# Linear attention with a highway layer on one core: softmax work of batches 2 and 3 moved, x added on GpSimd, output tiles as fp16 transposes

## Chip, core and metric

The kernel runs on one core of a Trainium2 chip. The metric is the device time of one execution in microseconds (us). A core has five engines with instruction queues of their own, each worked off in order: TensorE (PE, matrix products; its weight loads are PEld), VectorE (DVE), ScalarE (ACT), GpSimd (POOL) and SyncE (SP, which here only issues transfers). They wait for one another through semaphores. SBUF is the working memory of 128 partitions, PSUM the memory that PE writes to.

## What is computed

q, k and v have 8 batches, 8 heads, 576 rows and 64 columns. The result of the attention is, row by row, the input x of a highway layer with two 512 x 512 weight matrices.

```
q_s = exp(q) / sum over the 64 columns         # softmax of each row of a head
k_s = exp(k) / sum over the 576 rows
kv  = einsum('bhsd,bhse->bhde', k_s, v)        # one 64 x 64 matrix per head
x   = einsum('bhsd,bhde->bhse', q_s, kv)       # as 4608 rows of 512
H   = max(x @ w_h, 0)
T   = sigmoid(x @ w_t + b_t)
out = T * H + (1 - T) * x
```

Inputs and output are float32. Inside, the kernel works in fp16 with sums in fp32.

## The kernel before

**Layout.** A partition holds 9 consecutive rows (n = 0 to 8) of half of the heads, so a batch's q, k or v is one tile of 128 partitions x 2304 elements (1152 KB). A "half" a is half of the heads (1152 elements). x is kept transposed: xT[g] holds two batches (a group g) with the 512 model columns in four blocks of 128 (index k_ or ob) and rows n = 0 to 7. The ninth rows of all batches are collected in x9 and handled as a ninth "batch" at the end.

**Attention part of a batch b.** exp_half (L150) is the exponential on ACT, for q into eq and for k into ek. q_sums (L195) sums eq's rows on DVE, q_recip (L203) takes the reciprocals, and eq is scaled by them on GpSimd (q_scale_p, L214; the first 1024 elements, then 1280) or on DVE (q_scale_v, L206, which first widens the reciprocals, L210, and then multiplies, L212). cast_v (L160) brings half of v to fp16 on GpSimd. q_trans (L218) transposes scaled eq on PE in three pieces into PSUM (pq), copied to qsT on DVE (L233). kv_half (L167) is 36 small products of ek and v into psk; kv_norm (L183) divides by the key sums on DVE (rz, kvn). x_pair (L235) and x_left (L259) are the products px and px_l that give x; of an x_pair's copies into xT three of four are on ACT (L255), one on DVE (L257).

**Highway part of batch c and output block ob.** gate (L283) is four products with w_t into pt and a tanh on ACT in place. carry (L291) is four products with w_h into ph, then dd = max(ph, 0) - x on DVE (L297). blend (L302) is g = (tanh + 1) * dd on DVE (L305); since sigmoid(z) = (1 + tanh(z/2))/2, the output is x + g/2. out_tile (L321) brings one n of a group back to rows on PE: turn_block (L313) multiplies x by an identity and adds g times half an identity, both into fp32 PSUM (nat), eight products in all; ACT copies 512 elements (L336, in the last group every second tile on DVE, L334), and every fourth tile is followed by a transfer of 1 MB (L339). most9 and last9 (L347, L361) do the same for the ninth rows.

**Order.** The order of every queue is written out by hand. A list (L427 on) gives the start: batches 0 and 1 of attention, the weights, the four gates and carries of batch 0, and the loads of batches 2 and 3. After it, time runs in half steps p = 8 to 72, and `at(p, ...)` puts work on a half step. In each batch of 8 half steps a gate is at the even and a carry at the odd ones; blend(c, ob) is two half steps after its gate. The attention of batch b is placed relative to p = 8(b-1), where the gates of batch b-1 begin (L397 to L423). What is put on one half step is issued in the order in which it was put there, and each engine runs its share in that order.

**Buffers.** PSUM has four tiles for pt and ph (`ps_ht`), three for pq, psk, px and px_l (`ps_q`, in rotation) and one for nat (`ps_nat`). eq and ek have two buffers, q, k and v three each as loaded.

Of the kernel before, what the change touches and what calls it, by code (L numbers as in the profile page):

```python
# [18 lines left out]
def kernel(  # L19
# [86 lines left out]
    def cast_weight(n, k_, eng):  # L106
        o, i = w16[n][:, k_], w32[n][:, k_]
        if eng is nc.scalar:
            eng.copy(o, i)
        else:  # L110
            eng.tensor_copy(o, i)
# [47 lines left out]

    def cast_v(b, a, eng=None):  # L160
# [34 lines left out]
    def q_sums(b, a):  # L195
        if a == 0:
            qsum[b] = small.tile([P, N9, 4], FP32, tag="r32", name=f"r32_{b}")
        h = slice(2 * a, 2 * a + 2)
        nc.vector.reduce_sum(qsum[b][:, :, h], eq[b][:, :, h, :], axis=AX.X)  # L199

# [90 lines left out]
    def carry(c, ob):  # L291
        xv = views(c)[0]
        ps = ps_ht.tile([P, 8, 64], FP32, tag="ht", name=f"ph_{c}_{ob}")
        for k_ in range(4):
# [3 lines left out]
            dd, ps, 0.0, xv(ob), op0=ALU.max, op1=ALU.subtract  # L298
# [10 lines left out]

    o32 = {}  # L310
    rows = out.rearrange("(g p n) m -> g p n m", g=B // 2, n=N9)

    def turn_block(t, k_, xs, us):  # L313
        dst = t[:, k_, :]
        mm(dst, xs, ident, True, False)
        mm(dst, us, half_i, False, True)
# [4 lines left out]
    def out_tile(g, n, spare=False):  # L321
        if n % 4 == 0:
            o32[g, n // 4] = og.tile([P, 4, 512], FP32, tag="o32", name=f"o32_{g}_{n}")
        ps, tag = (ps_q, "qx") if spare and n % 4 < 3 else (ps_nat, "nat")
        t = ps.tile([P, 4, P], FP32, tag=tag, name=f"nat_{g}_{n}")
        for k_ in range(4):
            turn_block(
                t, k_,
                xT[g][:, k_, n].rearrange("p b d -> p (b d)"),
                gT[g][:, k_, n].rearrange("p b d -> p (b d)"),  # L330
            )
        o = o32[g, n // 4][:, n % 4, :]
        if spare and n % 2:
            nc.vector.tensor_copy(o, flat(t))  # L334
        else:
            nc.scalar.copy(o, flat(t))  # L336
        if n % 4 == 3:
            i = n // 4
            nc.sync.dma_start(rows[g][:, 4 * i : 4 * i + 4, :], o32[g, i])  # L339
# [43 lines left out]
    for c in range(1, B + 1):  # L383
        for ob in range(4):
            at(8 * c + 2 * ob + 2, E(blend, c, ob))

    for g in range(B // 2):
        p = 16 * (g + 1)
        if g < B // 2 - 1:
            for i in range(8):  # L390
                at(p + 2 + 2 * i, E(out_tile, g, i))
        else:
            for i in range(8):
                at(p + 1 + i // 2, E(out_tile, g, i, True))
    at(8 * B + 8, E(most9), E(last9))

    for b in range(2, B):  # L397
        p = 8 * (b - 1)
        s = p + {2: 0, 3: -4}.get(b, -5)
        at(s, E(exp_half, b, "q", 0))  # L400
        at(s + 1, E(exp_half, b, "q", 1), E(q_sums, b, 0))
# [88 lines left out]
```

## Time and profile before

| | us |
|---|---|
| median of 13 runs (148.53 to 151.34) | 149.09 |
| profiled execution, its own time | 149.08 |
| its span, first to last instruction | 146.9 |
| PE busy (share of the span) | 123.2 (84%) |
| DVE busy | 108.1 (74%) |
| ACT busy | 87.3 (59%) |
| POOL busy | 43.2 (29%) |
| mean granted TensorE clock | 0.966 |

The span leaves out 2.18 us that lie around the instructions. Busy times of engines overlap, so they don't add up to the span; a row such as "L216 POOL TENSOR_TENSOR eq<-eq,r" is a group of instructions by line, engine, operation and tiles, with total busy time and the mean of one. What an engine waited for is named by the instruction that released it. Matmuls are pipelined, so the mean duration of one (219 ns for 128 columns) is longer than the spacing of two that follow one another (0.056 us in the timeline).

### The profile page before, as it was taken

The page shows a single profiled execution, that of the slowest core. Times are in us where ns is not written, and L with a number is a line of the kernel's source. Part 1 is how long each engine was busy: PE and PEld are TensorE (multiplying, and loading weights), DVE is VectorE, ACT ScalarE, POOL GpSimd, SP SyncE. Part 2 cuts the span into 40 slices and gives each one's busy share as a digit, 9 for nine tenths or more (in the row PEclk, how much of TensorE's full clock was granted, in tenths as well). Part 3 has the DMA queues.
Part 4 walks back from the last instruction along what each step waited for, and adds up shares of the span by engine and source line. Part 5 has one row for each costly group of instructions (what it writes and reads, how often), then busy time and mean ns, then how long its engine had stood idle before and what let it go on. Part 6 is the DMA issues. An engine that isn't in the chain of part 4 may idle for free.

```text
span 146.9 us, 3530 instructions
## 1 busy us (share of the span) xinstructions
PE 123.2 (84%) x1477; PEld 67.9 (46%) x1477; DVE 108.1 (74%) x201; ACT 87.3 (59%) x126; POOL 43.2 (29%) x37
## 2 busy tenths in 40 slices
PE   4979999688528979979999599959977999999920
PEld 1335345234124436636645364634645455577620
DVE  1493589975997988996899389929983767577750
ACT  3650658336980269798499539936980764465420
POOL 2006011600084069059207900970295000000000
PEclk9999999999965999999999999999999999999995
DMA  4999999999999999403999999630051006047745
GB/s 156 354 383 408 410 391 410 412 413 405 412 408 411 407 411 411 173 0 140 271 407 414 324 405 407 280 154 0 4 225 62 4 0 285 0 174 319 297 176 181
DMA packets 16022, 40.06 MB, mean 273 GB/s; under 512 B 644, under 2 KB 1672, under 8 KB 14984
## 3 DMA queue, kind: packets, MB, share of 16 engines
q1 hardware_dynamic: 16008, 39.85, 70.6%
q8 instruction: 11, 0.18, 0.5%
q14 instruction: 3, 0.02, 0.0%
HBM read 30.41 MB, written 9.44 MB: 271 GB/s over the span
## 4 chain that ended last, share of the span: by engine, by line
PE 45%; DVE 29%; ACT 6%; POOL 6%; issue 4%; DMA 3%; POOLq 3%; SPq 0%; DVEq 0%; ACTq 0%
PE ph L59 14%; PE pt L59 12%; DVE r L199 10%; PE nat L59 6%; DVE dd L297 4%; PE psk L59 4%; POOL eq L216 3%; DVE eq L212 3%; DMA q<-in_q_dram 3%; DVE g L305 3%; POOLq L485 3%; PE pq L64 3%; PE px L59 3%; PE warm L59 3%; DVE qsT L233 2%
## 5 line engine op out<-in xcount | busy, mean ns | idle before, releaser
L288 ACT ACTIVATE pt<-pt,bt 128x512 f32<-128x512 f32 x36 | 24.0, 669 | 36.1 <-PE pt L59 35.7
L216 POOL TENSOR_TENSOR eq<-eq,r 128x1024 f16<-128x1024 f16 (+1 forms) x11 | 22.9, 2097 | 47.2 <-DVE r L204 34.6
L297 DVE SCALAR_TENSOR_TENSOR dd<-ph,xT 128x512 f16<-128x512 f32 x32 | 21.9, 684 | 16.9 <-PE ph L59 16.9
L59 PE MATMUL ph<-xT,w16h 128*128 128x512 f16 x128 | 33.7, 388 | 0.0
L59 PE MATMUL pt<-xT,w16t 128*128 128x512 f16 x128 | 32.9, 381 | 0.0
L305 DVE SCALAR_TENSOR_TENSOR g<-pt,dd 128x512 f16<-128x512 f32 x36 | 24.5, 681 | 1.9
L199 DVE TENSOR_REDUCE r<-eq 128x18 f32<-128x1152 f16 x16 | 21.6, 1348 | 4.4 <-ACT eq L154 4.1
L161 POOL CAST v<-v 128x1152 f16<-128x1152 f32 x16 | 18.6, 1185 | 13.8 <-DMA v<-in_v_dram 13.8
L154 ACT ACTIVATE ek<-k 128x1152 f16<-128x1152 f32 x16 | 18.6, 1184 | 2.5 <-DMA k<-in_k_dram 2.5
L154 ACT ACTIVATE eq<-q 128x1152 f16<-128x1152 f32 x16 | 18.4, 1171 | 2.6 <-DMA q<-in_q_dram 2.6
L59 PEld LDWEIGHTS <-w16t 128*128 128x128 f16 x144 | 12.8, 98 | 14.2 <-issue 1.1
L59 PE MATMUL nat<-half_i,g 128*128 128x128 f16 x140 | 18.7, 219 | 0.0
L59 PEld LDWEIGHTS <-w16h 128*128 128x128 f16 x144 | 12.4, 99 | 12.1 <-issue 1.7
L336 ACT COPY o<-nat 128x512 f32<-128x512 f32 x28 | 16.9, 602 | 1.7 <-issue 1.1
L64 PE MATMUL pq<-ident,eq 128*128 128x128 f16 x144 | 12.8, 231 | 6.0 <-POOL eq L216 4.1
L255 ACT CAST xT<-px 128x512 f16<-128x512 f32 x24 | 13.4, 596 | 7.2 <-PE px L59 7.1
L59 PE MATMUL nat<-ident,xT 128*128 128x128 f16 x128 | 17.3, 219 | 0.0
L59 PE MATMUL warm<-wide,ident 128*128 128x512 f16 x52 | 15.2, 441 | 1.9 <-DVE wide L140 1.9
L59 PEld LDWEIGHTS <-g 128*128 128x128 f16 x144 | 14.1, 98 | 3.8 <-DVE g L305 0.4
L64 PEld LDWEIGHTS <-eq 128*128 128x128 f16 x144 | 9.9, 103 | 9.8 <-POOL eq L216 4.6
L59 PEld LDWEIGHTS <-xT 128*128 128x128 f16 x128 | 12.5, 98 | 3.3
L59 PE MATMUL psk<-v,ek 64*64 64x65 f16 x576 | 8.1, 197 | 6.8 <-POOL v L161 5.5
(42 smaller groups left out, 91.7 us busy)
## 6 DMA issues: line engine op xcount, KB each, us to landing
out_dram<-o SPq DMA_DIRECT2D x8, 1024.0 KB, 4.3
q<-in_q_dram SPq DMA_DIRECT2D x7, 1152.0 KB, 13.4
k<-in_k_dram SPq DMA_DIRECT2D x7, 1152.0 KB, 14.3
v<-in_v_dram SPq DMA_DIRECT2D x6, 1152.0 KB, 14.7
v<-in_v_dram SPq DMA_DIRECT2D x4, 576.0 KB, 10.8
q<-in_q_dram SPq DMA_DIRECT2D x2, 576.0 KB, 4.1
k<-in_k_dram SPq DMA_DIRECT2D x2, 576.0 KB, 7.4
w32t<-in_moe_w_t_dram SPq DMA_DIRECT2D x1, 1024.0 KB, 13.7
```

Of the source, the lines that this page charges most:

```text
L59: mm = lambda o, l, r, st, sp: nc.tensor.matmul(o, l, r, start=st, stop=sp, skip_group_check=True)
L64: nc.tensor.matmul(o, i, ident, is_transpose=True, start=True, stop=True, skip_group_check=True,)
L154: nc.scalar.activation(dst[b][:, :, 2 * a : 2 * a + 2, :], in32[which][b][:, 2 * a : 2 * a + 2].rearrange("p c n d -> p n c d"), AF.Exp,)
L161: (eng or nc.gpsimd).tensor_copy(v16s[b % 2][:, :, 2 * a : 2 * a + 2, 0:64], in32["v"][b][:, 2 * a : 2 * a + 2].rearrange("p c n d -> p n ...
L199: nc.vector.reduce_sum(qsum[b][:, :, h], eq[b][:, :, h, :], axis=AX.X)
L212: nc.vector.tensor_mul(e, e, r2.unsqueeze(2).broadcast_to([P, w, 32, 2]))
L216: nc.gpsimd.tensor_mul(e, e, r.broadcast_to(list(e.shape)))
L255: nc.scalar.copy(dst, t[c])
L288: nc.scalar.activation(ps, ps, AF.Tanh, bias=bt2[:, ob : ob + 1], scale=0.5)
L297: nc.vector.scalar_tensor_tensor(dd, ps, 0.0, xv(ob), op0=ALU.max, op1=ALU.subtract)
L305: nc.vector.scalar_tensor_tensor(gv(ob), th, 1.0, dd, op0=ALU.add, op1=ALU.mult)
L336: nc.scalar.copy(o, flat(t))
```

## The change

1. **Weights.** w_h becomes (w_h - I)/2: four subtractions of the 128 x 128 identity blocks on DVE, and the casts on GpSimd and ACT multiply by 0.5.
2. **Carry.** dd = max(-x/2, ph), which with the new weights is half of the old dd. g is then the whole difference between output and x.
3. **add_x.** g += x on GpSimd, one instruction of 512 elements for each block of batches 0 to 7, one half step after its blend.
4. **Output.** out_pair replaces out_tile: two n at a time, eight fp16 transposes of g into one fp16 PSUM tile, one copy of 1024 elements, on ACT or, in the last group, every second one on DVE. The ninth rows keep two products each, with the whole identity.
5. **Softmax.** From batch 3 on, exp_all does a whole tile at once and q_sums_all sums by two fp16 additions and a reduction of the last 16 columns. All scales of batches 2 and up are on GpSimd.
6. **Order.** Batch 2's exponentials of q start ahead of the half steps, its v is cast half on GpSimd and half on DVE, its scales are at half steps 8 and 9; batch 3's softmax follows later than before; kv_half is at half steps 3 and 4 of most batches (4 and 5 of batch 4). The loads of batches 2 and 3 are written earlier in the list; SP's order stays the same.

```diff
     def cast_weight(n, k_, eng):
         o, i = w16[n][:, k_], w32[n][:, k_]
+        if n == "t":
+            eng.tensor_copy(o, i)
+            return
+
+        d = slice(k_ * P, k_ * P + P)
+        nc.vector.tensor_sub(i[:, d], i[:, d], ident)
         if eng is nc.scalar:
-            eng.copy(o, i)
+            eng.mul(o, i, 0.5)
         else:
-            eng.tensor_copy(o, i)
+            eng.tensor_scalar_mul(o, i, 0.5)
     for w in "qkv":
         load(0, w, [nc.sync, nc.sync])
...
             dst[b][:, :, 2 * a : 2 * a + 2, :],
             in32[which][b][:, 2 * a : 2 * a + 2].rearrange("p c n d -> p n c d"),
             AF.Exp,
+        )
+
+    def exp_all(b, which):
+        dst, p_ = {"k": (ek, ekp), "q": (eq, eqp)}[which]
+        dst[b] = p_.tile([P, N9, 4, 64], FP16, tag="e", name=f"e{which}_{b}")
+        nc.scalar.activation(
+            dst[b], in32[which][b].rearrange("p c n d -> p n c d"), AF.Exp
         )
     def cast_v(b, a, eng=None):
...
             qsum[b] = small.tile([P, N9, 4], FP32, tag="r32", name=f"r32_{b}")
         h = slice(2 * a, 2 * a + 2)
         nc.vector.reduce_sum(qsum[b][:, :, h], eq[b][:, :, h, :], axis=AX.X)
+
+
+    t32 = consts.tile([P, N9 * 4, 32], FP16, name="t32")
+    t16 = consts.tile([P, N9 * 4, 16], FP16, name="t16")
+
+    def q_sums_all(b):
+        qsum[b] = small.tile([P, N9, 4], FP32, tag="r32", name=f"r32_{b}")
+        e = eq[b].rearrange("p n c d -> p (n c) d")
+        nc.vector.tensor_add(t32, e[:, :, 0:32], e[:, :, 32:64])
+        nc.vector.tensor_add(t16, t32[:, :, 0:16], t32[:, :, 16:32])
+        nc.vector.reduce_sum(
+            qsum[b].rearrange("p n c -> p (n c)"), t16, axis=AX.X
+        )
     NG = [(0, 4), (4, 8), (8, 9)]
...
             mm(ps, w16["h"][:, k_, ob * P : ob * P + P], xv(k_), k_ == 0, k_ == 3)
         dd = mo.tile([P, 8, 64], FP16, tag="dd", name=f"dd_{c}_{ob}")
         nc.vector.scalar_tensor_tensor(
-            dd, ps, 0.0, xv(ob), op0=ALU.max, op1=ALU.subtract
+            dd, xv(ob), -0.5, ps, op0=ALU.mult, op1=ALU.max
         )
         live[c, ob] = (live[c, ob], dd)
...
         )
+    def add_x(c, ob):
+        xv, gv = views(c)
+        nc.gpsimd.tensor_add(gv(ob), gv(ob), xv(ob))
+
+
     o32 = {}
     rows = out.rearrange("(g p n) m -> g p n m", g=B // 2, n=N9)
     def turn_block(t, k_, xs, us):
         dst = t[:, k_, :]
         mm(dst, xs, ident, True, False)
-        mm(dst, us, half_i, False, True)
+        mm(dst, us, ident, False, True)
     def flat(t):
         return t.rearrange("p k d -> p (k d)")
-    def out_tile(g, n, spare=False):
-        if n % 4 == 0:
-            o32[g, n // 4] = og.tile([P, 4, 512], FP32, tag="o32", name=f"o32_{g}_{n}")
-        ps, tag = (ps_q, "qx") if spare and n % 4 < 3 else (ps_nat, "nat")
-        t = ps.tile([P, 4, P], FP32, tag=tag, name=f"nat_{g}_{n}")
-        for k_ in range(4):
-            turn_block(
-                t, k_,
-                xT[g][:, k_, n].rearrange("p b d -> p (b d)"),
-                gT[g][:, k_, n].rearrange("p b d -> p (b d)"),
-            )
-        o = o32[g, n // 4][:, n % 4, :]
-        if spare and n % 2:
-            nc.vector.tensor_copy(o, flat(t))
+    def out_pair(g, i, spare=False):
+        if i % 2 == 0:
+            o32[g, i // 2] = og.tile([P, 4, 512], FP32, tag="o32", name=f"o32_{g}_{i}")
+        ps, tag = (ps_q, "qx") if spare and i < 3 else (ps_nat, "nat")
+        t = ps.tile([P, 2, 512], FP16, tag=tag, name=f"nat_{g}_{i}")
+        for j in range(2):
+            for k_ in range(4):
+                ptrans(
+                    t[:, j, k_ * P : k_ * P + P],
+                    gT[g][:, k_, 2 * i + j].rearrange("p b d -> p (b d)"),
+                )
+        h = i // 2
+        o = o32[g, h][:, 2 * (i % 2) : 2 * (i % 2) + 2, :]
+        if spare and i % 2:
+            nc.vector.tensor_copy(o, t)
         else:
-            nc.scalar.copy(o, flat(t))
-        if n % 4 == 3:
-            i = n // 4
-            nc.sync.dma_start(rows[g][:, 4 * i : 4 * i + 4, :], o32[g, i])
+            nc.scalar.copy(o, t)
+        if i % 2:
+            nc.sync.dma_start(rows[g][:, 4 * h : 4 * h + 4, :], o32[g, h])
     rows9 = out.rearrange("(g p n) m -> n p g m", g=B // 2, n=N9)[NM]
...
     for c in range(1, B + 1):
         for ob in range(4):
             at(8 * c + 2 * ob + 2, E(blend, c, ob))
+            if c < B:
+                at(8 * c + 2 * ob + 3, E(add_x, c, ob))
     for g in range(B // 2):
         p = 16 * (g + 1)
-        if g < B // 2 - 1:
-            for i in range(8):
-                at(p + 2 + 2 * i, E(out_tile, g, i))
-        else:
-            for i in range(8):
-                at(p + 1 + i // 2, E(out_tile, g, i, True))
+        for i in range(4):
+            if g < B // 2 - 1:
+                at(p + 3 + 4 * i, E(out_pair, g, i))
+            else:
+                at(p + 3 + i, E(out_pair, g, i, True))
     at(8 * B + 8, E(most9), E(last9))
+    at(8, E(q_sums, 2, 1), E(q_recip, 2), E(cast_v, 2, 0), E(q_scale_p, 2, 0, 4))
+    at(9, E(exp_half, 2, "k", 0), E(q_scale_p, 2, 4, N9))
+    at(10, E(exp_half, 2, "k", 1))
+    at(11, E(cast_v, 2, 1, nc.vector))
     for b in range(2, B):
         p = 8 * (b - 1)
-        s = p + {2: 0, 3: -4}.get(b, -5)
-        at(s, E(exp_half, b, "q", 0))
-        at(s + 1, E(exp_half, b, "q", 1), E(q_sums, b, 0))
-        at(s + 2, E(q_sums, b, 1), E(q_recip, b), E(q_scale_p, b, 0, 4))
-        if b == 2:
-            at(s + 3, E(q_scale_v, b, 4, N9))
-        else:
-            at(s + 3, E(q_scale_p, b, 4, N9))
-        s = p + {2: 2, 3: 0}.get(b, -1)
-        at(s, E(exp_half, b, "k", 0))
-        at(s + 1, E(exp_half, b, "k", 1))
-        s += b == 2
-        at(s, E(cast_v, b, 0))
-        at(s + 1, E(cast_v, b, 1))
+        if b > 2:
+            s = p + {3: -2, 4: -4}.get(b, -5)
+            at(s, E(exp_all, b, "q"))
+            at(s + 1, E(q_sums_all, b))
+            at(s + 2, E(q_recip, b))
+            if b > 3:
+                at(s + 2, E(q_scale_p, b, 0, 4))
+                at(s + 3, E(q_scale_p, b, 4, N9))
+            s = p + {3: 0, 4: 0}.get(b, -1)
+            at(s, E(exp_all, b, "k"), E(cast_v, b, 0))
+            at(s + 1, E(cast_v, b, 1))
+            if b == 3:
+                at(p + 1, E(q_scale_p, b, 0, 4), E(q_scale_p, b, 4, N9))
         tr, kv, x = {
-            2: ((4, 4, 5), (5, 6), (7, 7, 7)),
-            3: ((2, 3, 4), (4, 5), (6, 6, 7)),
-        }.get(b, ((2, 3, 4), (2, 3), (4, 5, 6)))
+            2: ((4, 5, 5), (3, 4), (6, 7, 7)),
+            3: ((4, 5, 5), (3, 4), (6, 7, 7)),
+            4: ((2, 3, 4), (4, 5), (6, 6, 7)),
+        }.get(b, ((2, 3, 4), (3, 4), (5, 6, 7)))
         for i in range(3):
             at(p + tr[i], E(q_trans, b, i))
         at(p + kv[0], E(kv_half, b, 0))
...
         E(q_trans, 1, 0), E(q_trans, 1, 1), E(q_trans, 1, 2),
         E(gate, 0, 2), E(carry, 0, 2), E(blend, 0, 2),
         E(kv_half, 1, 0), E(gate, 0, 3), E(kv_half, 1, 1), E(kv_norm, 1),
-        E(carry, 0, 3),
+        E(carry, 0, 3), *[E(load, b, w) for b in (2, 3) for w in "qkv"],
+        E(exp_half, 2, "q", 0),
         E(x_pair, 1, 0), E(x_pair, 1, 1), E(blend, 0, 3), E(x_left, 1),
-        *[E(load, b, w) for b in (2, 3) for w in "qkv"],
+        E(exp_half, 2, "q", 1), E(q_sums, 2, 0),
+        *[E(add_x, 0, ob) for ob in range(4)],
     ]:
         f()
     for p in range(8, 8 * (B + 1) + 1):
...
```

## The prediction

> **What bounds the kernel now.** I read the slices first, then busy time by stage, then who waited for whom, then the chain. By the slices TensorE (PE) is the fullest engine, yet its share is an average over stages with different limits, so I cut the span at the first gate product of each batch (34.3, 53.2, 65.6, 77.5, 91.3, 105.1, 119.1, 127.8 us, read in the timeline). Columns: stage, its length, busy time of PE, weight loads, VectorE (DVE), ScalarE (ACT), GpSimd (POOL), granted clock, DMA share, GB/s.
>
> ```profile
> 34.30:53.20 18.90, 12.97 (x142) 6.42 (x140) 16.53 (x26) 10.48 (x13) 5.25 (x4) 0.82 1.04 410
> 77.50:91.30 13.80, 11.97 (x172) 7.04 (x171) 10.98 (x21) 10.05 (x16) 6.37 (x4) 1.00 1.03 386
> 119.10:127.80 8.70, 8.70 (x66) 4.92 (x64) 5.54 (x8) 4.70 (x8) 0.00 (x0) 1.00 0.29 121
> ```
>
> Three regimes: a start and a batch-2 stage in which PE idles about 6 us and runs at a lower clock; a steady stage of 13.8 us per batch with PE idle 1.8 us in each; a tail in which PE never stops. The waits name what ends last (us in total, times, longest):
>
> ```profile
> PE psk L59 <- POOL v L161: 5.5, 3, 1.8
> PE pq L64 <- POOL eq L216: 4.1, 1, 4.1
> POOL eq L216 <- DVE r L204: 34.6, 5, 7.5
> ```
>
> and the chain (start, us, what) shows one turn of the steady loop:
>
> ```profile
> 77.52 0.39 DVE r L204
> ...
> 79.93 2.33 POOL eq L216
> 82.27 1.10 POOL v L161
> 83.41 0.48 PE psk L59 x34
> ...
> 91.34 0.39 DVE r L204
> ```
>
> From the end of one reciprocal (77.90) GpSimd scales the queries (4.14), casts half the values (1.10), and PE's psk product starts at 83.41: 5.51 us. From there gate or carry, qsT, rz, kvn, two reductions and the next reciprocal end at 91.72: 8.31 us. 5.51 + 8.31 = 13.82, the period. So GpSimd, busy 6.4 of 13.8 us, is on the loop that sets the period.
>
> **What the Trainium skill says.** "SBUF — State Buffer", Who interferes with whom: a VectorE instruction with two SBUF inputs, or in a two-port mode, and a GpSimd instruction that reads SBUF lock each other out, whole instruction by whole instruction. The trace agrees: with GpSimd busy from 40.93 to 45.6, an L210 cast took 1.66 us instead of 0.18 and an L212 product 1.69 instead of 0.82. "GPSIMD Engine Reference", 3.1: a two-input operation reads both operands through one port, about 2.6 cycles an element. Here it is cheaper, 1.68 ns an element (rows below), but twice the cast's 0.83, as a shared port would give. "VectorE: DVE Perf Modes", the perf-mode tier table: 16-bit tensor_tensor runs at 2x, tensor_reduce at 1x. Agrees: 1024 elements in 0.69 (L212), 1152 in 1.35 (L199). "TensorE: Matmul & The Clock Gate", Part 1: an idle window of about 3.4 us halves the clock. Agrees: after 4.12 us without work (38.8 to 42.9) the carry's matmuls at 45.5 came 0.43 us apart instead of 0.22.
>
> Rows for prices (busy, mean ns, idle before):
>
> ```profile
> L216 POOL TENSOR_TENSOR eq<-eq,r 128x1280 f16<-128x1280 f16 x5 | 11.7, 2331 | 0.0
> L216 POOL TENSOR_TENSOR eq<-eq,r 128x1024 f16<-128x1024 f16 x6 | 11.4, 1902 | 47.2 <-DVE r L204 34.6 <-ACT ek L154 12.6
> L111 POOL CAST w16h<-w32h 128x512 f16<-128x512 f32 x2 | 1.2, 616 | 7.3 <-DMA w32h<-in_moe_w_h_dram 7.3
> L59 PE MATMUL nat<-ident,xT 128*128 128x128 f16 x128 | 17.3, 219 | 0.0
> L199 DVE TENSOR_REDUCE r<-eq 128x18 f32<-128x1152 f16 x16 | 21.6, 1348 | 4.4 <-ACT eq L154 4.1
> L336 ACT COPY o<-nat 128x512 f32<-128x512 f32 x28 | 16.9, 602 | 1.7 <-issue 1.1 <-ACT o L336 0.6
> ```
>
> **Prices of the new operations.** add_x (512 elements, two inputs, GpSimd): slope (2331-1902)/256 = 1.68 ns, fixed 1902-1024x1.68 = 0.18 us, so 1.04 us. Ends: 0.62 (the 512-element one-input cast) and 1.2 (2.6 cycles). Tree of sums: t32 0.76 and t16 0.46 from L212's 0.69 for 1024 at 2x, last reduction 1.35-576/960 = 0.75; 1.97 instead of 2.69, about 1.9 after overlap. exp_all: 1.17 + 1152x0.83 ns = 2.1, little less than two halves (2.2). Output pair: eight products at the 0.056 us spacing of nat, 0.45 us, for what took 0.90; the copy of 1024 elements on ACT 0.60+0.43 = 1.03 against 1.20, on DVE about 1.2 against 1.38. dd with its operands exchanged: same shape, one SBUF input as before, 0.68. Weight subtraction: 0.25 each on DVE (between 0.2, a 128x128 tensor_scalar, and 0.29, kvn).
>
> **Start.** DVE ends the scaling of batch 1 at 25.13. Four subtractions follow, meeting GpSimd's multiplications on the shared port; the last w16h block is ready at about 27.2, where the old casts ended at 22.7, unneeded until DVE was free. carry(0,0), the dd behind it and the q_trans and kv products queued behind on PE all slip; psk of batch 1 starts at 31.45 instead of 29.18, the first gate of batch 1 at 36.7 instead of 34.28. +2.4 us. The loads keep SP's order, so data arrive as before; loads of batch 6 wait behind an output issued at about 65 (67.83 before) and are needed at about 87: nothing.
>
> **Batches 2 to 4.** exp_half(2) moves ahead, but its sums queue behind the late blend on DVE: reciprocal of batch 2 at about 40.55 (before 40.75). GpSimd then does both scales, to 44.8. The DVE cast of v (0.75) arrives at about 42.5, exactly as the second scale starts: it goes first, or waits 2.3 us. exp_all(3) (2.1) now stands on ACT ahead of the last xT copy of batch 2, which gate(2,0) needs. So gate(2,0) comes at 51.5 (53.3 if the cast waits; before 53.16): the 6 us of idle PE is mostly not recovered. In batch 3, x_left's copy waits for that xT copy, sums_all(3) for it, and blend(1,3) for both; add(1,3) holds cast_v(3,1) and the two scales behind it. gate(3,0) at 66.0 (before 65.6). GpSimd: scale, add, scale, cast, add, cast after the reciprocal of 65.7 puts kv_half(4,1) at 74.3; sums_all(5) meets adds on the port, reciprocal of batch 5 between 77.5 and 78.8. I take 78.2, plus half of the 1.5 us that a losing cast costs: 78.95. Before: 77.9. +1.05, with the start inside it.
>
> **The loop with the adds.** GpSimd's order per batch is scale, scale, add, cast, cast, add, add, add. Reciprocal to psk: 5.51 + 1.04 = 6.55. psk to the next reciprocal: psk, gate, pq, psk 2.2; rz, kvn 0.6; tree 1.95; dd 0.6; reciprocal 0.35: 5.7. Sum 12.25, plus 0.3 to 1.35 because t32 and t16 fall into two adds on the port; 0.8: 13.05 for batch 6. For batches 5 and 7 a new wait is last: out_pair(1,0) and out_pair(2,0) stand on PE in front of q_trans(.,1) and kv_half(.,0), and need add_x(.,3), which GpSimd reaches after both casts: 0.16+4.14+1.04+2.24+1.04 = 8.62, then the transposes left and pq, 0.8: psk at 9.4 after the reciprocal, all gates queued behind. Period 9.4+5.7 = 15.1. Reciprocal of batch 5 to psk of batch 7: 15.1+13.05+9.4 = 37.55; before 111.05-77.90 = 33.15. +4.4.
>
> **Tail.** From psk of batch 7 to the end of the last carry PE is the bound: before 27.7 (111.05 to 138.76). After: slots 52 to 71, twenty gate or carry groups at 0.866 = 17.3; seven pairs 3.15; psk, pq, px and their gaps 2.5: 22.95. -4.75. The adds (1.04 per 1.73 us) and copies fit beside it. The last 1 MB output is issued about 1.9 us later against the end; the 8.1 us behind the last carry grow by 0.4.
>
> **Sum.** 1.05 + 4.4 - 4.75 + 0.4 = +1.1. Against the profiled execution's own 149.08 (span 146.9 and 2.18 around it; the median, 149.09, is the same): 150.2. PE loses 7.2 us of work (128 products), and all but the tail's share lies where PE waits for GpSimd.
>
> **Rivals.** (1) Faster: the add costs less than two reads. Place: the loop from batch 5 on and its boundaries. At the cast's 0.62 each add gives back 0.42; five stand on the 37.55 us path and about three more in port collisions and ahead of batch 5: -3.4, and 0.8 of collisions goes: 146.0. It decides below about 0.9 us an add, where 1.1/8 = 0.14 is saved. For it: an all-16-bit form isn't in the trace. Against: the exact factor of two between L216 and the cast. (2) Slower still: PE waits about 4.7 us ahead of out_pair(2,0), longer than the 4.12 us after which the clock fell; then some 5 us at half rate cost 2.0 to 2.5, and the losing cast another 0.75: 153.3. Against: the 1.8 us waits cost no clock.
>
> **Chances.** Forecast 48%, range 148 to 152.5; rival 1 33%; rival 2 19%. A measurement can tell about 0.2%, 0.3 us, from no change. Forecast splits slower 0.38, same 0.06, faster 0.04; rival 1 faster 0.31, same 0.01, slower 0.01; rival 2 slower. Faster 0.35, same 0.07, slower 0.58. The range takes in most of both rivals: 145 to 154.5.
>
> **What would show it.** Right: first gate of batch 1 near 36.7; add_x near 1.04; PE waiting for GpSimd's adds in front of out_pair(1,0) and (2,0), 1.5 to 5 us; tail without idle PE, about 23 us from the last psk. Wrong: adds near 0.7, steady periods below 12.5 us on average, or a batch-2 stage under 13 us (34.3 to 53.2 before), which would take several us off my +1.05.

## The result, and the profile after

The changed kernel takes 155.36 us (median of 11 runs, 153.11 to 156.76), the kernel before 149.39 (48 runs): a ratio of 1.036, with an interval of 1.032 to 1.039. The forecast was 150.2 with a range up to 154.5: slower, as forecast, but by 6.0 us instead of 1.1. The profiled execution of the changed kernel took 153.42 us, of which 151.3 are its span. Its executions differ by the clock that TensorE was granted: 0.961 or 0.962 with spans of 151.3 to 152.3 us, 0.928 or 0.929 with spans of 153.5 to 154.6 us, and some between; the profiled one lies 1.9 us under the median. Ratios and their intervals, here and below, leave out executions that are over 1.5% above the fastest of the same kernel; medians leave out none.

The stages of batches 1, 5, 6 and 7, each from the first gate products of that batch to those of the next (for batches 2 and 6 the cut is at the last part of that gate, which waits). Columns: stage, its length, busy time of PE, weight loads, DVE, ACT, POOL, granted clock, DMA share, GB/s:

```profile
38.84:53.35 14.51, 11.42 (x144) 5.34 (x141) 12.56 (x25) 9.12 (x11) 11.35 (x8) 1.00 1.05 391
95.85:110.50 14.65, 12.10 (x166) 6.46 (x159) 12.41 (x25) 12.31 (x13) 12.43 (x9) 1.00 0.39 155
110.50:126.28 15.78, 12.25 (x151) 6.25 (x151) 8.89 (x19) 5.73 (x10) 10.63 (x9) 0.89 0.13 51
126.28:134.09 7.81, 7.81 (x56) 4.04 (x49) 5.57 (x11) 4.49 (x6) 3.86 (x4) 1.00 0.33 136
```

The first of them, which the prediction calls the batch-2 stage, shrank from 18.9 to 14.5 us, and the tail per batch from 8.7 to 7.8. But the first gate of batch 1 moved from 34.3 to 38.8, and the stages of batches 5 and 6 are 14.7 and 15.8 us, where they took 13.8 each. Those of batches 2, 3 and 4, which are not shown, took 13.8, 16.7 and 12.0 us (12.4, 11.9 and 13.8 before). GpSimd is busy 12.4 of 14.7 us, where it was busy 6.4 of 13.8.

Who waited for whom (total, times, longest):

```profile
POOL g L338 <- DVE g L331: 19.8, 13, 3.6
...
PE ph L59 <- POOL w16h L117: 4.6, 2, 4.2
...
PE nat L64 <- POOL g L338: 3.8, 3, 3.1
```

The two lines of PE are new. Two causes stand behind them: at the start PE waits for a weight block that GpSimd multiplies (L117), and ahead of output pairs it waits for GpSimd's additions of x (L338). The first line is GpSimd's own waiting for the blends; only 1.3 us of it lie between 60 and 118 us, so in the loop it seldom waits for a blend.

One turn of the loop in the chain (start, us, what), from the scaling of batch 5 to its psk:

```profile
80.26 4.17 POOL eq L242 x2
84.43 1.11 POOL g L338
85.54 2.18 POOL v L174 x2
87.72 1.12 POOL g L338
...
88.89 0.45 PE nat L64 x5
89.35 0.45 PE pq L64 x8
89.79 0.41 PE psk L59 x36
```

Where scale, cast and psk followed one another in 5.5 us before, the chain now runs through two additions and an output pair: scale, add, cast, cast, add, then the pair's transposes that waited for the last add, then pq, and only then psk, 9.7 us after the reciprocal. GpSimd doesn't stop between the scaling and the last of these additions.

The groups that answer to the prices (busy, mean ns of one):

```profile
L338 POOL TENSOR_TENSOR g<-g,xT 128x512 f16<-128x512 f16 x32 | 37.8, 1190 | 19.9 <-DVE g L331 19.8
...
L368 ACT CAST o<-nat 128x1024 f32<-128x1024 f16 x14 | 14.2, 1012 | 14.0 <-PE nat L64 12.8 <-issue 1.0
...
L221 DVE TENSOR_TENSOR t<-eq 128x1152 f16<-128x1152 f16 x5 | 5.3, 1058 | 1.0 <-ACT eq L169 1.0
L222 DVE TENSOR_TENSOR t<-t 128x576 f16<-128x576 f16 x5 | 4.0, 791 | 0.2
...
L117 POOL TENSOR_SCALAR w16h<-w32h 128x512 f16<-128x512 f32 x2 | 3.1, 1576 | 11.2 <-DVE w32h L113 11.2
```

The addition (priced at 1.04) has a mean of 1.19 and a median of 1.15. The two additions of halves (0.76 and 0.46) have these durations only where no GpSimd addition meets them; their means are 1.06 and 0.79. The multiplication of a weight block takes 1576 ns on GpSimd, where the cast of the same 512 elements took 616.

### The profile page after: what moved, and what is told of

It is laid out like the page before. It is cut to its first block, busy times and chain, and to the rows that moved or that the text cites. A ratio compares the mean times of both kernels' runs of the same rounds, so it can differ in the third digit from the quotient of the medians.

```text
span 151.3 us, 3294 instructions
## 1 busy us (share of the span) xinstructions
PE 119.9 (79%) x1349; PEld 60.4 (40%) x1349; DVE 106.7 (71%) x207; ACT 86.2 (57%) x102; POOL 83.4 (55%) x69
## 4 chain that ended last, share of the span: by engine, by line
PE 35%; POOL 25%; DVE 20%; issue 7%; ACT 6%; DMA 3%; SPq 0%; POOLq 0%; DVEq 0%; ACTq 0%
POOL eq L242 12%; PE pt L59 10%; PE ph L59 10%; POOL g L338 5%; POOL v L174 5%; DVE r L212 4%; PE nat L64 3%; DMA q<-in_q_dram 3%; PE psk L59 3%; PE pq L64 3%; PE warm L59 2%; ACT eq L160 2%; PE px L59 2%; DVE t L221 2%; POOL w16h L117 2%
## 5 line engine op out<-in xcount | busy, mean ns | idle before, releaser
L338 POOL TENSOR_TENSOR g<-g,xT 128x512 f16<-128x512 f16 x32 | 37.8, 1190 | 19.9 <-DVE g L331 19.8
L323 DVE SCALAR_TENSOR_TENSOR dd<-xT,ph 128x512 f16<-128x512 f16 x32 | 21.7, 677 | 9.9 <-PE ph L59 9.8
L368 ACT CAST o<-nat 128x1024 f32<-128x1024 f16 x14 | 14.2, 1012 | 14.0 <-PE nat L64 12.8
L259 DVE COPY qsT<-pq 128x1024 f16<-128x1024 f16 (+1 forms) x24 | 12.8, 552 | 10.5 <-PE pq L64 10.4
L59 PEld LDWEIGHTS <-w16t 128*128 128x128 f16 x144 | 12.7, 99 | 14.8 <-issue 3.6
L64 PE MATMUL nat<-ident,g 128*128 128x128 f16 x128 | 10.9, 225 | 3.8 <-POOL g L338 3.8
L64 PEld LDWEIGHTS <-g 128*128 128x128 f16 x128 | 8.9, 101 | 8.5 <-POOL g L338 4.4
L212 DVE TENSOR_REDUCE r<-eq 128x18 f32<-128x1152 f16 x6 | 8.0, 1349 | 4.3 <-ACT eq L160 4.2
L169 ACT ACTIVATE eq<-q 128x2304 f16<-128x2304 f32 x5 | 10.6, 2128 | 0.0
L169 ACT ACTIVATE ek<-k 128x2304 f16<-128x2304 f32 x5 | 10.6, 2122 | 0.0
L59 PE MATMUL px<-qsT,kvn 64*64 64x512 f16 x64 | 7.2, 398 | 3.5 <-DVE kvn L201 2.4
(50 smaller groups left out, 110.1 us busy)
## 6 DMA issues: line engine op xcount, KB each, us to landing
q<-in_q_dram SPq DMA_DIRECT2D x7, 1152.0 KB, 14.5
v<-in_v_dram SPq DMA_DIRECT2D x4, 576.0 KB, 11.2
```

The source lines that it names most:

```text
L59: mm = lambda o, l, r, st, sp: nc.tensor.matmul(o, l, r, start=st, stop=sp, skip_group_check=True)
L64: nc.tensor.matmul(o, i, ident, is_transpose=True, start=True, stop=True, skip_group_check=True,)
L169: nc.scalar.activation(dst[b], in32[which][b].rearrange("p c n d -> p n c d"), AF.Exp)
L323: nc.vector.scalar_tensor_tensor(dd, xv(ob), -0.5, ps, op0=ALU.mult, op1=ALU.max)
L338: nc.gpsimd.tensor_add(gv(ob), gv(ob), xv(ob))
L368: nc.scalar.copy(o, t)
```

## The experiments

A stands for "GpSimd's queue sets the time: the additions in the loop, the weight multiplication at the start", B for "the new softmax order and the sums by halves cost the time", C for "the waits cost little themselves, the clock falls after them do". All times are medians; ratios are to the kernel before in the same session.

**1. Without the additions.** The output of batches 0 to 7 lacks x.

```diff
-            if c < B:
-                at(8 * c + 2 * ob + 3, E(add_x, c, ob))
...
-        *[E(add_x, 0, ob) for ob in range(4)],
```

> The changed kernel without its 32 adds on GpSimd, so x is missing from the output of batches 0 to 7. Theory A (GpSimd's queue sets the loop: every add lengthens the way from a reciprocal to the next psk product, and output pairs wait behind the last add of a group): from the reciprocal of batch 5 to the psk of batch 7 38.6 us fall to 28 to 31, no wait of the output pairs for GpSimd, time 143 to 147 us instead of 155.4. Rival B (the rearranged softmax of batches 2 to 7 and its two-input sums cost the time, the adds run in GpSimd's idle time): 152 to 155. Rival C (only the clock that falls in PE's longest waits): 152 to 154.

Measured: 143.38 us (140.40 to 144.29), 12.0 under the changed kernel. The psk products of batches 5, 6 and 7 start at 87.5, 98.7 and 110.1 us, 11.2 and 11.4 apart; in the changed kernel at 89.7, 102.0 and 118.6, 12.3 and 16.6 apart. A's time of 143 to 147 us holds; from the reciprocal of batch 5 to the psk of batch 7 there are 31.7 us, a little over A's 28 to 31. The 32 additions are the largest single cost. Between the two profiled executions, which differ by 10.1 us, 6.3 us arise between psk of batch 5 and psk of batch 7.

**2. Output pairs two half steps later.** The additions stay; only the place in PE's order at which the pairs of groups 0 to 2 stand is moved.

```diff
-                at(p + 3 + 4 * i, E(out_pair, g, i))
+                at(p + 5 + 4 * i, E(out_pair, g, i))
```

> Output pairs of groups 0 to 2 two half steps later, so that they stand behind the key/value products on PE instead of in front of them; no work is taken away. Theory A: the way from reciprocal to psk of batches 5 and 7 falls from 9.7 to 6.6 us, twice 3.1 us; with the longest idle time of PE gone, its clock stays up, another 1 to 2 us: 147 to 150 us. Rival B: within 1 us of 155.4. Rival C: 152 to 154 (clock alone).

Measured: 150.48 us (20 runs), ratio 1.005 (1.002 to 1.008), 4.9 less than the changed kernel and half a us over A's 147 to 150. The waits for additions ahead of output pairs are gone from the trace; what remains between GpSimd and psk is 1.3 us in two waits for the cast of v, and 0.2 in one for an addition. psk of batch 7 starts at 116.1 instead of 118.6. So some 5 of the 12 us that the additions cost come from the output pair that stands on PE between the additions and psk, not from their length.

**3. The output part alone**, on the softmax order of before.

```diff
-            at(s, E(exp_all, b, "q"))
-            at(s + 1, E(q_sums_all, b))
...
+        at(s, E(exp_half, b, "q", 0))
+        at(s + 1, E(exp_half, b, "q", 1), E(q_sums, b, 0))
...
-        }.get(b, ((2, 3, 4), (3, 4), (5, 6, 7)))
...
+        }.get(b, ((2, 3, 4), (2, 3), (4, 5, 6)))
```

> The kernel before with parts 1 to 4 of the change alone (weights less identity, half dd, adds on GpSimd, output pairs), softmax and its order as before. Theory A: start 4.5 us later, the loop longer by about 4 to 5 us, tail shorter by 4: 153 to 157 us. Rival B: these parts alone shed 7 us of PE work and are harmless: 145 to 149.

Measured: 164.74 us (164.16 to 165.03), ratio 1.101 (1.092 to 1.110): slower than A's 153 to 157 by 8 us, and far from B's range. The wait that names it, and one of the periods:

```profile
PE psk L59 <- POOL v L174: 11.8, 4, 3.4
```

```profile
89.36:106.00 16.64, 12.91 (x156) 7.14 (x155) 10.98 (x22) 10.10 (x13) 10.84 (x8) 0.90 0.85 301
```

In the old order psk stands a half step earlier on PE, PE waits for the cast of v in each of four batches, and the granted clock falls to 0.90 in this period and in the next one, of 16.4 us. The direction is A's; its size was foreseen by neither. The output part costs 15.2 us on this order (164.74 against 149.56 in the same session) and 14.5 on the new one (155.36 against 140.85 of experiment 4), so the two parts of the change hardly help or hinder one another.

**4. The softmax parts alone**, with weights, dd and output as before.

```diff
-        at(s, E(exp_half, b, "q", 0))
-        at(s + 1, E(exp_half, b, "q", 1), E(q_sums, b, 0))
...
+            at(s, E(exp_all, b, "q"))
+            at(s + 1, E(q_sums_all, b))
...
-        }.get(b, ((2, 3, 4), (2, 3), (4, 5, 6)))
...
+        }.get(b, ((2, 3, 4), (3, 4), (5, 6, 7)))
```

> The kernel before with parts 5 and 6 alone (whole-tile exponentials, sums by additions, order of batches 2 to 7), output as before. Theory A: batch 2's stage about as long, the loop shorter by the cheaper sums and the later products (PE-bound near 12 us a batch, as GpSimd has no adds): 142 to 148 us. Rival B: the loss is here, 153 to 156.

Measured: 140.85 us (139.87 to 141.49), ratio 0.942 (0.934 to 0.949), a little better than A expected. B is refuted: this part gains 8.5 us. Where the gain lies shows in a window of the loop:

```profile
87.00:99.00 12.00, 12.00 (x172) 6.96 (x171) 10.46 (x24) 10.12 (x14) 6.38 (x4) 1.00 0.66 255
```

PE is busy in all of these 12.0 us, at full clock, and psk of batches 5, 6 and 7 follow one another every 12.0 us (13.8 before). The loop through GpSimd is no longer the bound: of PE's 5.5 us of waits for the cast of v, whose psk now stands a half step later, 0.2 are left. Whether the later psk or the shorter sums do more of it was not tried apart.

**5. The start of the weights.** The subtractions go ahead of the scaling of batch 1, the multiplications all to ScalarE.

```diff
-        d = slice(k_ * P, k_ * P + P)
-        nc.vector.tensor_sub(i[:, d], i[:, d], ident)
...
+    def less_ident(k_):
+        i, d = w32["h"][:, k_], slice(k_ * P, k_ * P + P)
+        nc.vector.tensor_sub(i[:, d], i[:, d], ident)
...
-        E(q_sums, 1, 1), E(q_recip, 1), E(q_scale_v, 1, 0, 4), E(q_scale_v, 1, 4, N9),
-        *[E(cast_weight, "h", k_, (nc.gpsimd, nc.scalar)[k_ % 2]) for k_ in range(4)],
+        E(q_sums, 1, 1), E(q_recip, 1), *[E(less_ident, k_) for k_ in range(4)],
+        E(q_scale_v, 1, 0, 4), E(q_scale_v, 1, 4, N9),
+        *[E(cast_weight, "h", k_, nc.scalar) for k_ in range(4)],
```

> The changed kernel; the four weight subtractions stand ahead of the scaling of batch 1 on VectorE, and all four multiplications by 0.5 run on ScalarE (0.63 us each in the trace of the changed kernel) and none on GpSimd (1.58 us each). A (the start is lost to the weights, above all to GpSimd's two multiplications): the last w16h block is ready near 26 us instead of 28.5, TensorE's wait for it (4.2 us) shrinks below 3 us, the first gate product of batch 1 comes at 35.5 to 37 us instead of 38.8, and the median falls by 1.5 to 3 us. B (the start is slow because the softmax work of batch 2 was moved into it): the first gate stays within 0.7 us of 38.8 and the median within 1 us.

Measured: 151.28 us (20 runs), ratio 1.006 (1.003 to 1.010): 4.1 less, more than A's 1.5 to 3. First the wait in the changed kernel (PE's timeline: start, us, idle before in brackets), then the multiplications in this one:

```profile
27.09 1.04 PE L59 MATMUL ph<-xT,w16h 128*128 128x512 f16 x2 [4.22 <-POOL w16h L117]
28.54 2.37 PE L59 MATMUL ph<-xT,w16h 128*128 128x512 f16 x6 [0.42 <-POOL w16h L117]
```

```profile
L113 ACT ACTIVATE w16h<-w32h 128x512 f16<-128x512 f32 x4 | 2.2, 620 | 3.5 <-DVE w32h L119 3.5
```

Four multiplications on ScalarE take 2.2 us, where two on GpSimd took 3.1; the subtractions take 0.27 each there instead of 0.39; PE's wait for w16h falls from 4.6 to 1.2 us, and the first gate of batch 1 comes at 35.35 instead of 38.84. The edit does two things: the subtractions begin 1.8 us earlier (23.19 instead of 24.99), and the last block follows the first multiplication's start by 2.2 us instead of 3.1. The two weren't tried apart.

**6. The additions on VectorE.**

```diff
-        nc.gpsimd.tensor_add(gv(ob), gv(ob), xv(ob))
+        nc.vector.tensor_add(gv(ob), gv(ob), xv(ob))
```

> The changed kernel with the 32 additions of x on VectorE instead of GpSimd, in the same places of the order. A (the adds cost by their place in GpSimd's queue, 1.0 to 1.2 us each there): an addition of 512 16-bit elements takes about 0.35 to 0.45 us on VectorE, the reciprocal of batch 6 to its psk shrinks from 6.6 to about 5.5 us, the waits ahead of the output pairs to under 1.5 us, and the time is 145 to 149 us. B (any engine with these adds is too full, or the added work as such costs): no gain over 2 us against the changed kernel, and VectorE is busy over 85% in the stages from batch 5 on.

Measured: 153.60 us (152.23 to 153.86), ratio 1.026 (1.018 to 1.034). A's 145 to 149 is missed, and both of B's signs are there: a gain under 2 us, and a VectorE that is busy over 85%.

```profile
L338 DVE TENSOR_TENSOR g<-g,xT 128x512 f16<-128x512 f16 x32 | 20.4, 645 | 0.0
...
L174 DVE CAST v<-v 128x1152 f16<-128x1152 f32 x1 | 2.9, 2947 | 0.0
```

```profile
106.00:118.00 12.00, 11.36 (x153) 5.92 (x152) 11.86 (x26) 9.11 (x11) 6.24 (x4) 1.00 0.22 90
```

The median of an addition is 0.42 us, as expected, but beside GpSimd's work one takes up to 1.89, and the mean is 0.65. In these 12.0 us VectorE is busy 11.86. Yet the loop itself does what A says: from psk of batch 5 to psk of batch 7 it takes 24.5 us, where the changed kernel takes 28.9. The gain is lost ahead of it. The stage of batch 1, between the first gate products of batches 1 and 2, takes 17.0 us instead of 13.1: VectorE has the additions of batch 0 and 1 there, and the cast of v of batch 2 on VectorE, which came 2.1 us later, met GpSimd's scaling and took 2.95 us instead of 0.87, the case that the prediction had put at 2.3 us of waiting. PE waited 2.5 us for it. Additions on VectorE with that cast elsewhere weren't tried.

**7. Work in PE's waits**, to hold the clock.

```diff
+    again = {(6, 1): 4, (4, 1): 1}
...
+        for _ in range(again.get((c, ob), 0)):
+            for k_ in range(4):
+                mm(ps, w16["h"][:, k_, ob * P : ob * P + P], xv(k_), k_ == 0, k_ == 3)
```

> The changed kernel with useless repeats of one carry's products (four times at carry(6,1), once at carry(4,1)), which fill the stretches in which TensorE waits for GpSimd ahead of the output pairs; nothing else differs. C (clock falls after these waits cost time): the granted clock stays at full rate through the last two batches and the tail, and the median falls by 1 to 2.5 us. A alone (the waits cost, the clock hardly): the repeats are hidden, and the median stays within 0.8 us of the changed kernel, or grows by up to 1 us.

Measured: 153.85 us (152.64 to 154.26), ratio 1.028 (1.020 to 1.036). The row of granted clock (40 slices of the span, tenths), of the changed kernel and of this one:

```profile
PEclk9999999599999999999997799999999779999998
```

```profile
PEclk9999999689999999999999699999999999999995
```

The fall at the last wait (slices 32 and 33) is gone; the two before it, near 27 and 82 us, stay. Between psk of batch 7 and the end of the last carry this execution takes 22.8 us, where the changed kernel took 24.3: the fall cost 1.5 us in that stretch. But psk of batch 5 comes 0.8 us later than there, and that delay stays, so that the span gains only 0.7. The median is 1.5 us lower, at the small end of C, but the two ratios' intervals overlap: the times of these four runs don't separate C from A.

**8. One reduction in place of the sums by halves.**

```diff
-        nc.vector.tensor_add(t32, e[:, :, 0:32], e[:, :, 32:64])
-        nc.vector.tensor_add(t16, t32[:, :, 0:16], t32[:, :, 16:32])
-        nc.vector.reduce_sum(
-            qsum[b].rearrange("p n c -> p (n c)"), t16, axis=AX.X
-        )
+        nc.vector.reduce_sum(qsum[b], eq[b], axis=AX.X)
```

> The changed kernel with the sums of batches 3 to 7 as one reduction of 2304 elements instead of two additions of halves and a short reduction. If the additions of halves lock out GpSimd's adds (they took 1.06 and 0.79 us instead of 0.76 and 0.46, and the adds 1.19 instead of 1.04): GpSimd's adds come nearer to 1.04 us on average, the reduction takes 2.6 to 2.7 us, as much as the three together did, and the median stays within 1 us. If they don't: the adds keep their 1.19, the sums get longer by 0.1 to 0.7 us a batch on the path, and the median grows by 0.5 to 3 us.

Measured: 153.99 us (153.69 to 155.45), ratio 1.032 (1.024 to 1.041), the same as the changed kernel within the interval.

```profile
L330 POOL TENSOR_TENSOR g<-g,xT 128x512 f16<-128x512 f16 x32 | 36.6, 1153 | 21.5 <-DVE g L323 21.5
...
L217 DVE TENSOR_REDUCE r<-eq 128x36 f32<-128x2304 f16 x5 | 12.7, 2549 | 1.0 <-ACT eq L169 1.0
```

One reduction takes 2.55 us, the three operations together took 1.06 + 0.79 + 0.75 = 2.60; and beside it no addition takes over 1.17 us, where one took 1.68. So, next to GpSimd's additions, the sums by halves gain nothing: what two-input operations save, they lose on the port. The first expectation holds, except that an addition is 1.15 us by itself, not 1.04.

**9. Edits 2 and 5 together.**

```diff
-                at(p + 3 + 4 * i, E(out_pair, g, i))
+                at(p + 5 + 4 * i, E(out_pair, g, i))
...
+        E(q_sums, 1, 1), E(q_recip, 1), *[E(less_ident, k_) for k_ in range(4)],
+        E(q_scale_v, 1, 0, 4), E(q_scale_v, 1, 4, N9),
+        *[E(cast_weight, "h", k_, nc.scalar) for k_ in range(4)],
```

> The changed kernel with both single edits: the weight subtractions ahead of the scaling of batch 1 with all four multiplications on ScalarE (alone: 151.28 us against 155.36), and the output pairs of groups 0 to 2 two half steps later (alone: 150.48 us). A (two separate losses, the start and the waits ahead of the output pairs): the gains of 4.1 and 4.9 us add up, and the median is 145.5 to 147.5 us. C (both edits gain the same thing, since either removes waits after which the clock falls): they don't add up, and the median is 148 to 150.5 us.

Measured: 146.01 us (144.76 to 147.51), ratio 0.976 (0.970 to 0.981). The gains add up: 155.36 - 4.1 - 4.9 = 146.4. This version, with all parts of the change, is 2.4% faster than the kernel before.

**10. Edits 1 and 5 together.** Again x is missing from the output of batches 0 to 7.

```diff
-            if c < B:
-                at(8 * c + 2 * ob + 3, E(add_x, c, ob))
...
+        E(q_sums, 1, 1), E(q_recip, 1), *[E(less_ident, k_) for k_ in range(4)],
+        E(q_scale_v, 1, 0, 4), E(q_scale_v, 1, 4, N9),
+        *[E(cast_weight, "h", k_, nc.scalar) for k_ in range(4)],
...
-        *[E(add_x, 0, ob) for ob in range(4)],
```

> The changed kernel with the start of the weights mended in the same way, and without the 32 additions of x (batches 0 to 7 of the output lack x). A: of the 143.4 us without the additions, another 3 to 4 us go with the start, and the median is 139 to 140.5 us, about the 140.85 us of the kernel before with the softmax parts alone: then the additions and the start are the whole cost of the output part. If it stays over 142 us, the output part costs more than these two.

Measured: 138.56 us (136.32 to 140.48), ratio 0.920 (0.914 to 0.927). With the start mended and without additions, the output part gains 2.3 us on experiment 4. The time is a little under A's 139 to 140.5. The additions and the start are its whole cost.

**11. The output part in the tail only**, on experiment 4: a second set of weights for batches 6 and 7, x added for these two, and only the last group leaves as pairs.

```diff
+    def second_weight(k_):
...
+        nc.vector.tensor_scalar_mul(o, w16["h"][:, k_], 0.5)
+        nc.vector.tensor_sub(o[:, d], o[:, d], half_i)
...
+            if c in (B - 2, B - 1):
+                at(8 * c + 2 * ob + 3, E(add_x, c, ob))
+    for k_ in range(4):
+        at(46 + k_ // 2, E(second_weight, k_))
...
-            for i in range(8):
-                at(p + 1 + i // 2, E(out_tile, g, i, True))
+            for i in range(4):
+                at(p + 3 + i, E(out_pair, g, i, True))
```

> The kernel before with the softmax parts (140.85 us alone), and the output part for the last group only: w16h/2 less half the identity is made on VectorE in a free buffer for batches 6 and 7, x is added on GpSimd for these two batches only, after its last softmax work, and the last group leaves as four pairs of 16-bit transposes; groups 0 to 2 leave as before. A (the additions cost only because they stand in GpSimd's queue among the softmax work): TensorE, which never stops in the tail, loses 8 x 0.45 = 3.6 us of work, and the time is 136.5 to 138.5 us. B (the output part costs wherever it is put): 140 us or more.

Measured: 146.98 us, ratio 0.987 (0.984 to 0.991), 6.1 more than experiment 4. By its number B would have won, but the trace tells of another cause, the experiment's own. VectorE's timeline and the wait on PE show it:

```profile
98.30 1.76 DVE L319 TENSOR_SCALAR w2h<-w16h 128x512 f16<-128x512 f16 x1
100.09 2.23 DVE L320 TENSOR_TENSOR w2h<-w2h,half_i 128x128 f16<-128x128 f16 x1
102.25 1.23 DVE L319 TENSOR_SCALAR w2h<-w16h 128x512 f16<-128x512 f16 x1
103.52 1.04 DVE L320 TENSOR_TENSOR w2h<-w2h,half_i 128x128 f16<-128x128 f16 x1
...
105.69 0.28 DVE L319 TENSOR_SCALAR w2h<-w16h 128x512 f16<-128x512 f16 x1
106.00 0.23 DVE L320 TENSOR_TENSOR w2h<-w2h,half_i 128x128 f16<-128x128 f16 x1
```

```profile
105.22 0.59 PE L59 MATMUL pt<-xT,w16t 128*128 128x512 f16 x1 [5.99 <-DVE xT L276]
```

The same two operations take 0.28 and 0.23 us once GpSimd has ended, and 1.0 to 2.2 while it scales and casts batch 7 (98.0 to 104.5). An xT copy stood behind them, and PE waited 6.0 us for it. "SBUF — State Buffer", Who interferes with whom, in the Trainium skill says that such instructions lock each other out, whole instruction by whole instruction, and the run agrees: four small operations that need 1.0 us took 6.3.

**12. The same without that mistake:** ScalarE halves dd for batches 6 and 7, and there is no second set of weights.

```diff
+        if c in (B - 2, B - 1):
+            nc.scalar.mul(dd, dd, 0.5)
```

> As the kernel with pairs in the tail alone (146.98 us), but without the second set of weights, whose eight small VectorE operations fell into GpSimd's scaling of batch 7 and took 7.0 us there instead of about 2; for batches 6 and 7 ScalarE halves dd instead (eight times about 0.6 us, in its idle time of the tail). The gain expected before (3.6 us) was counted twice over: four pairs save 4 x 0.45 = 1.8 us. A (additions that stand behind the last softmax work cost nothing): TensorE doesn't wait in the last two batches, and the time is 138.3 to 139.8 us, against 140.85 for the softmax parts alone. B (the output part costs wherever it is put): 140.5 us or more.

Measured: 139.38 us (139.10 to 144.54), ratio 0.932 (0.929 to 0.934), as A expected, and faster than both kernels. The intervals of this and of experiment 4 just touch.

```profile
106.00:131.00 25.00, 24.55 (x219) 14.00 (x204) 18.51 (x32) 16.74 (x29) 7.56 (x7) 1.00 0.36 148
```

PE doesn't wait for GpSimd here: the eight additions lie behind its last cast, and PE's only idle time from 99 to 131 us, 0.45 us, is for VectorE. From psk of batch 7 to the last block of output takes 26.7 us (103.69 to 130.44) instead of 28.0 (105.27 to 133.28): 1.3 of the 1.8 us expected. These eight additions, of a kind that the loop pays for, cost PE no waiting here.

## Why the prediction was right or wrong

By experiments 4, 10, 1 and the changed kernel, the 6.0 us are made up so: the softmax parts gain 8.5 us (149.4 to 140.85), the output part with neither its start nor its additions another 2.3 (to 138.56), the start of the weights costs 4.8 (to 143.38) and the additions 12.0 (to 155.36). The softmax parts alone give the first number, and the start alone (experiment 5, 4.1 us) roughly the third. The four runs of experiments 1 and 10 spread over 4 us each, so that the parts taken from them are known to about 1 or 2 us only; by the fastest run of each kernel the four parts are 8.7, 3.6, 4.1 and 12.7 us.

The forecast missed by 5.2 us. By the profiled execution 1.1 of them had arisen at the reciprocal of batch 5, from the start, 1.05 arose in the loop and 1.35 in the tail; 1.9 lie between that execution and the median. Three steps of the prediction failed: GpSimd's multiplications of the weights were given no price of their own, the clock of the tail was put at nothing, and the profiled time was taken for the median.

The prediction's own terms, against the profiled execution (us):

| term | predicted | measured |
|---|---|---|
| first gate of batch 1 | 36.7 | 38.84 |
| end of the reciprocal of batch 5 | 78.95 | 80.08 |
| from there to psk of batch 5 | 9.4 | 9.71 |
| psk to the end of the next reciprocal | 5.7 | 5.65 |
| to psk of batch 6 | 6.55 | 6.59 |
| psk to the next reciprocal | 6.5 | 6.94 |
| to psk of batch 7 | 9.4 | 9.71 |
| psk of batch 7 to the end of the last carry | 22.95 | 24.3 |
| behind it | 8.5 | 8.3 |
| span | 148.0 | 151.3 |

**The loop with the additions** was right in mechanism and nearly in size: the new wait ahead of the output pairs, the place of each addition in GpSimd's order, 38.6 us from reciprocal to psk against 37.55. The missing 1.05 us is the addition (1.15 to 1.19 instead of 1.04) and 0.44 us where the sums by halves met two additions, which I had put at 0.8 and which took 1.3 (1.24 and 1.29 us instead of 0.76 and 0.46). Experiments 1, 2 and 9 confirm it.

**The start** was mis-sized: its +2.4 has a price for the four subtractions, but none for a multiplication on GpSimd, whose cast took 0.62. The step "four subtractions follow, meeting GpSimd's multiplications on the shared port; the last w16h block is ready at about 27.2" gave the multiplications no price of their own. They take 1.58 us each, and the last block was ready at 28.5. PE waited 4.2 us ahead of the first products and 0.4 more ahead of the last six, which took 2.37 us at a clock of 0.61, where four take 1.04 at the full one. That wait is longer than the 4.12 us after which the prediction had seen the clock fall; it put no loss there. The first gate came 2.1 us later than forecast: 1.3 of them are the late block, most of the rest is the clock. At the reciprocal of batch 5 there are 1.1 left of it, but 78.95 held 0.75 for a cast that might lose the port and didn't: against the 78.2 without it, 1.9 of the 2.1 us are still there. The median gains 4.1 us when the start is mended (experiment 5).

**The tail** was right in its work (PE never waits in it, 7.8 us per batch) and wrong by 1.35 us in its clock. That is the mechanism of rival 2: PE stood still for 3.5 us ahead of out_pair(2,0), with one product in between, not the 4.7 us assumed, and its clock was at half rate from 119.2 to 122.6. Without that fall the stretch took 22.8 us in experiment 7. Two places in PE's timeline of the changed kernel:

```profile
79.65 0.62 PE L59 MATMUL px<-qsT,kvn 64*64 64x512 f16 x5 [2.35 <-DVE kvn L201]
...
117.78 0.45 PE L64 MATMUL nat<-ident,g 128*128 128x128 f16 x5 [3.06 <-POOL g L338]
...
119.02 1.80 PE L59 MATMUL pt<-xT,w16t 128*128 128x512 f16 x4
```

Four gate products take 1.80 us instead of 1.04. I gave this 19%, arguing that waits of 1.8 us had cost no clock; between 1.8 and 4.1 the profile before had no case. The first line shows one: after a wait of 2.35 us the clock was at half rate as well, from 81.6 to 85.0, at a place where GpSimd, not PE, was on the path. The other half of rival 2, the cast of v that loses the port, did not happen: 0.87 us, though it did when the cast came 2.1 us later (experiment 6). Rival 2's number, 153.3, is near the profiled 153.4 by accident: the start makes up what the cast did not cost.

**The median** lies another 1.9 us above the profiled execution; its runs at a clock of 0.928 instead of 0.962 are the longer ones. I had set the profiled time equal to the median because it was so before. Which wait brings the clock down in which execution stays open; experiment 7 took one fall away and left the others.

**Rival 1** (a cheap addition, 0.62) is refuted by the 1.15 us. **Batches 2 to 4** were close: gate(2,0) began at 51.98, and its last part, which waited for the xT copy behind exp_all(3), came at 53.35 (51.5 forecast for the whole); gate(3,0) began at 67.14 (66.0). Both have the late start in them. **Prices** that held: the output copy 1.01 on ACT and 1.22 on DVE (1.03 and 1.2), the pair's products 0.45, exp_all 2.12 (2.1), the last reduction 0.75.

**What the sum hid**: added up along one path, it never showed that the change is two changes of opposite sign, -8.5 and +14.5 us, which by experiment 3 nearly add up. The first, which takes PE's wait for the cast out of the loop, was not costed by itself; doing so would have shown PE as the bound at 12.0 us a batch, and every later wait for GpSimd as a loss against that.

## What to carry to other kernels

Work that is moved from the fullest engine to one that is half idle is paid for when that engine's queue lies on the loop: here 7.2 us of PE's products became 38 us of GpSimd additions, part of them in front of the casts that the next batch waits for, and cost 12 us. Eight of these additions, put behind the last work of that queue, made PE wait for nothing. Split a change of several parts into those that can stand alone, and cost each by itself before adding them up. Price every operation that changes its form, also where it looks like the one that it replaces (a multiplication for a cast), and ask of any new wait on TensorE what the products behind it will cost at half clock: in these traces 2 to 3 us of waiting were mostly enough for that.

## What the runs showed of the hardware

- GpSimd's multiplication by a constant, 512 elements from 32 to 16 bits, took 1.58 us on average and 1.49 with VectorE idle; its cast of the same elements took 0.62, ScalarE's multiplication 0.62 to 0.63.
- An addition of two 16-bit operands of 512 elements took 1.15 us on GpSimd and 0.42 on VectorE alone; beside GpSimd's work VectorE's took up to 1.89. A reduction of one operand on VectorE left GpSimd's additions at 1.15.
- Half rate after a wait came in stretches of 3.4 us or of twice that, and at no fixed time: in the changed kernel at the end of a wait of 4.2 us (27.0), 1.9 us after the end of one of 2.35 (81.6) and 1.4 us after the end of one of 3.1 (119.2). In all traces, behind the first 20 us, it began in or soon behind eight of nine waits of 2.1 to 2.7 us, behind none of the three of 1.8 us in the kernel before, and not behind the last of experiment 3, of 3.2 us; in experiment 4 it began at 48.7 us, where the waits just before were of 0.7 and 0.8 us. "TensorE: Matmul & The Clock Gate", Part 1, in the Trainium skill speaks of an idle window of about 3.4 us; the stretches have that length here, but single waits that are shorter were enough, so that below that length one wait by itself doesn't tell whether the clock will fall.
